# One written order for the first steps of a layer norm, Fourier mixing and MLP kernel; the copies of x moved behind the first transposes

## The chip, the cores and the metric

The kernel runs on one core of a Trainium2 chip. The metric is the device time of one execution in microseconds (us); before the change three runs gave a median of 1219.32 us. Five engines take part, each with its own queue that it works off in order: PE (TensorE, matmuls and the transposes made with matmuls), DVE (VectorE), ACT (ScalarE), POOL (GpSimd), and SP, which issues DMAs. POOL issues DMAs too.

## What is computed

```python
x = A_x                                   # 2048 x 576, f32
xn = _layernorm(x, axis=-1)
a, b = xn @ dft_hid_re.T, xn @ dft_hid_im.T
y = dft_seq_re @ a - dft_seq_im @ b       # 2048 x 2048 matrices
h = relu(xn @ w1)                         # w1: 576 x 4608
out = x + y + h @ w2                      # w2: 4608 x 576
```

Every f32 operand is carried as two f16 numbers, a high part and a low part (the value less its high part), and a product is three f16 matmuls (high by high, high by low, low by high). The products of the second layer and of the Fourier part are made in 2 x 2 blocks with seven multiplications instead of eight, which is why there are sums and differences of blocks as well.

## The kernel before

The 2048 rows of x are 16 tiles of 128 rows, tile 0 to 15, in four groups of four. The 4608 columns of the hidden layer are nine blocks of 512, taken as two pairs of 256. The main loop runs over steps `n` = (block `b`, group `g`), 36 of them: in step n the first layer of (b, g) and the second layer of the step before it stand interleaved. This change concerns what comes before step n = 3, that is block 0 with groups 0, 1 and 2.

A tile of x goes through this path. Its mean and variance (`stats`: two `bn_stats`, one `bn_aggr`, a square root on ACT, four short DVE operations). The normalized f32 value (`normalize`, L302 on DVE or L300 on ACT) and its f16 high part (L303 on ACT). The low part (`remainder`, L309 and L312, 64 and 512 columns, on POOL or DVE). Then ten 128 x 128 transposes: tiles 0 to 3 with matmuls (`transposes`, L332 and L336) and two copies out of PSUM on ACT (`copies`, L343 and L346); tiles 4 to 15 with one transposing DMA each from SP (`transposes_dma`, L326), for which 128 columns are copied once more first (L324 on POOL or L322 on ACT). Normalized tiles share four buffers in turn (tile t takes buffer t modulo 4).

The weights: `max_w1` and `power_w1` find a power-of-two scale of a block of w1, `split_w1` (L230 high, ACT; L231 low, DVE) makes the two f16 parts; `sum_w2`, `power_w2`, `split_w2`, `sums_w2` do it for w2. A scale needs a maximum over the 128 partitions. In block 0 that goes over PE (`power_pe`). In every later block it is POOL's `partition_all_reduce` (L168), after which DVE makes the scale (L171, L172, L176) and ACT and DVE the parts. In the middle of the first steps stands one more such reduction, of a constant into a tile that nobody reads (L1003, tile `none`).

The first layer of group 0 and half of group 1 is made tile by tile (`tile_by`, 14 matmuls of 128 columns), the rest with 512 columns (`mlp1`, L388). `mlp1_out` and `pair_out` make the f16 parts of the relu values and of their sums (L441 to L464); their last operation, on DVE, is the low part of four sums (L464). `mlp2` makes seven products a group (L699, 12 matmuls each, two PSUM banks in turn), ACT or DVE takes them out (L714, L718), and POOL adds four finished quarters to DRAM tiles `spill` with an accumulating DMA (L721). Those tiles start as copies of x (`copy_x`, L909).

What sets the order. Before step 3, each engine's queue is arranged by a scheduler from the order in which the code stands and from extra constraints (`behind(key)`: not before a named instruction). From step 3 on nearly everything goes through `pinned`, which lets an instruction follow the one that was issued before it on PE, ACT and DVE. `fill(n)` puts matmuls on PE whose result is not used. `work()` takes the next piece of the preparation of block 1 from a list (`prepare_block(1)`).

Of the kernel before, what the change touches and what calls it, by code (L numbers as in the profile page):

```python
# [18 lines left out]
P = 128  # L19
S = 2048  # L20
D = 576
# [34 lines left out]
def kernel(  # L56
# [142 lines left out]
    def power_pe(s, p, m):  # L199

        n = m.shape[-1]
        ps = ps2.tile([P, 2, 512], F32, tag="ps2", name="pm")

        for c in range(n):
            nc.tensor.matmul(
                ps[:1, 0, c * P : (c + 1) * P], m[:, c : c + 1], ident.bitcast(BF16),
                start=True, stop=True,
            )
        top = small.tile([1, n], BF16, tag=f"top{n}", name="top")
        order["top"] = nc.vector.tensor_reduce(  # L210
            top, ps[:1, 0, : n * P].rearrange("p (n f) -> p n f", f=P), AX.X, ALU.max
        ).ins
        order["pm"] = nc.tensor.matmul(ps[:, 1, :n], ones, top, start=True, stop=True).ins
        half = small.tile([P, n], F32, tag=f"half{n}", name="half")
        nc.vector.tensor_scalar(half, ps[:, 1, :n], 2.0**-107, 2.0**6, ALU.max, ALU.mult)
        nc.vector.tensor_scalar(
            s.bitcast(I32), half.bitcast(I32), EXPONENT, EXPONENT,
            ALU.bitwise_and, ALU.bitwise_xor,
        )
        nc.vector.tensor_scalar(  # L220
            p.bitcast(I32), half.bitcast(I32), EXPONENT, None, ALU.bitwise_and
        )
# [4 lines left out]
    def split(hi, lo, src, s):  # L227

        return (
            nc.scalar.activation(hi, src, AF.Copy, scale=s).ins,  # L230
            nc.vector.scalar_tensor_tensor(lo, src, s, hi, ALU.mult, ALU.subtract).ins,  # L231
        )
# [15 lines left out]
    def stats(ts, after=None, late=None):  # L248

        n = len(ts)  # L250
        mv = small.tile([P, n, 2], F32, tag=f"mv{n}", name=f"mv{ts[0]}")
        sts = [small.tile([P, 2, 6], F32, tag="st", name=f"st{t}", bufs=4) for t in ts]
        for t, st in zip(ts, sts):
            for j in range(2):
                with behind(after):
                    nc.vector.bn_stats(st[:, j, :], acc[t][:, j * EH : (j + 1) * EH])  # L256
                yield
        for i, st in enumerate(sts):
            order["stats"] = nc.vector.bn_aggr(mv[:, i], st.rearrange("p a b -> p (a b)")).ins
            yield  # L260
        r0, u, r, sh = (
            small.tile([P, n], F32, tag=f"{a}{n}", name=f"{a}_{ts[0]}") for a in ("r0", "u", "r", "sh")
        )
        m, v = mv[:, :, 0], mv[:, :, 1]
        stt = nc.vector.scalar_tensor_tensor
        order["root", ts[0]] = nc.scalar.activation(u, v, AF.Sqrt, bias=eps, scale=HALF**2).ins
        with behind(late):
            nc.vector.reciprocal(r0, u)
            stt(r0, v, EPS, r0, ALU.add, ALU.mult)
        yield  # L270
        with behind(late):
            stt(r0, r0, HALF**2, u, ALU.mult, ALU.add)
        yield
        with behind(late):
            nc.vector.reciprocal(r, r0)
        yield
        with behind(late):
            order["sh", ts[0]] = stt(sh, m, -1.0, r, ALU.mult, ALU.mult).ins
        for i, t in enumerate(ts):
            means[t], factors[t], shifts[t] = mv[:, i, 0:1], r[:, i : i + 1], sh[:, i : i + 1]  # L280

    def weave(steps, *others):

        others = list(others)
        for _ in steps:
            if others:
                others.pop(0)()
        for f in others:
            f()
# [3 lines left out]
    def normalize(t, eng=nc.vector, after=None):  # L293
        stage = dbufs[t % 4]
        xn = xns[t] = stage[:, :D]

        xs = xss[t] = stage[:, D : 2 * D + P // 2].bitcast(F16)
        with behind(after):
            if eng is nc.scalar:
                nc.scalar.activation(xn, acc[t], AF.Identity, bias=shifts[t], scale=factors[t])  # L300
            else:
                eng.tensor_scalar(xn, acc[t], means[t], factors[t], ALU.subtract, ALU.mult)  # L302
            order["N", t] = nc.scalar.activation(  # L303
                xs[:, :D], acc[t], AF.Identity, bias=shifts[t], scale=factors[t]
            ).ins

    def remainder(t, eng):
# [4 lines left out]
        order["E", t] = eng.tensor_tensor(  # L312
            xs[:, D + REM : 2 * D], xn[:, : KM * P], xs[:, : KM * P], ALU.subtract
        ).ins

    def transposes_dma(t, eng):

        xs = xss[t]
        g, c = divmod(t, TG)
        again = xs[:, 2 * D :], xs[:, D - P : D]  # L320
        if eng is nc.scalar:
            eng.activation(*again, AF.Copy)  # L322
        else:
            order["again"] = eng.tensor_copy(*again).ins  # L324
        with behind("td"):
            order["td"] = nc.sync.dma_start_transpose(xT[g][:, :, c * P : (c + 1) * P], xs).ins  # L326

    def transposes(t):
        xs = xss[t]
        pt = ps2.tile([P, 2, 1024], F16, tag="ps2", name=f"pt{t}")  # L330
        for k in range(NKX):
            nc.tensor.transpose(  # L332
                pt[:, k // 8, (k % 8) * P : (k % 8 + 1) * P], xs[:, k * P : (k + 1) * P], ident
            )

        nc.tensor.transpose(pt[:, 1, P : 2 * P], xs[:, D - P : D], ident)  # L336
        return pt

    def copies(t, pt, after=None):
        g, c = divmod(t, TG)  # L340
        dst = xT[g][:, :, c * P : (c + 1) * P]
        with behind(after):
            nc.scalar.activation(  # L343
                dst[:, :8, :], pt[:, 0, :].rearrange("p (k t) -> p k t", t=P), AF.Copy
            )
            nc.scalar.activation(  # L346
                dst[:, 8:, :], pt[:, 1, : 2 * P].rearrange("p (k t) -> p k t", t=P), AF.Copy
            )

# [70 lines left out]

    def mlp1_out(b, g, i, pa, pb, after=None, last=None, late=False):  # L430

        h, st = new_h(b, g, i), stages[i].rearrange("p (k t) -> p k t", t=GH)
        stt = nc.vector.scalar_tensor_tensor
        a11, a21, a12, a22 = pa[:, :GH], pa[:, GH:], pb[:, :GH], pb[:, GH:]
        r21, s1, s2, s3, s4 = (st[:, n] for n in range(5))
        with behind(after):  # L440
            nc.scalar.activation(r21, a21, AF.Relu)  # L441
        both = pb.rearrange("p (a t) -> p a t", t=GH)
        for q, src in ((A11, a11), (slice(A12, A22 + 1), both)):
            hi, lo = (h[:, n, q] for n in range(2))
            with behind(after):
                order["hi"] = nc.scalar.activation(hi, src, AF.Relu).ins
                order["hl"] = stt(lo, src, 0.0, hi, ALU.max, ALU.subtract).ins  # L447

        def values():
            with behind(last or after):  # L450
                stt(s3, a11, 0.0, r21, ALU.max, ALU.subtract)
                stt(s1, a22, 0.0, r21, ALU.max, ALU.add)
                stt(s2, a22, 0.0, s3, ALU.max, ALU.subtract)
                stt(s4, a12, 0.0, s2, ALU.max, ALU.subtract)

        hi, lo = (h[:, n, S1 : S4 + 1] for n in range(2))

        def high():
            with behind("free" if late else None):
                order["s"] = nc.scalar.activation(hi, st[:, 1:], AF.Copy).ins  # L460

        def low(key="vfree"):
            with behind(key if late else last):
                order["lo"] = nc.vector.tensor_tensor(lo, st[:, 1:], hi, ALU.subtract).ins  # L464

        if last:
            return lambda: (values(), high(), low())
        values()
        if late:
            return high, low  # L470
        high()
        low()

# [248 lines left out]
    def max_w1(b, f):  # L725
# [6 lines left out]
        with behind("vfree" if b else ("sh", 1) if f > 1 else None):  # L732
# [13 lines left out]
    def power_w1(b, i):  # L746
# [4 lines left out]
        else:  # L751
            power_pe(s, p, mx["b", i])

    def split_w1(b, f):
# [6 lines left out]
        split(w[:, 0, k], w[:, 1, k], raws["w1", b, i][:, k], sc["w1", b][:, i : i + 1])  # L761
# [22 lines left out]
    def sum_w2(b, i, after=("root", 4)):  # L784
# [5 lines left out]
        with behind("free" if b >= BB else None if b else after):  # L790
# [4 lines left out]
    def power_w2(b):  # L795
# [3 lines left out]
        else:  # L799
            m = small.tile([P, NQ], BF16, tag="mb2", name=f"mb2_{b}")  # L800
            with behind("stats"):
                order["cast"] = nc.vector.tensor_copy(m, mx["w2", b]).ins
            power_pe(sc["w2", b], pw["w2", b], m)
        p1 = pw["w1", b]
        pp = cell("pp")
        nc.vector.tensor_tensor(pp, p1, pw["w2", b], ALU.mult)
        m = cell("mp", 1)
        nc.vector.tensor_reduce(m, pp, AX.X, ALU.max)
        inv = cell("inv", 1)
        nc.vector.tensor_scalar(  # L810
            inv.bitcast(I32), m.bitcast(I32), EXPONENT, None, ALU.bitwise_xor
        )
        sc["w2", b] = cell("sw2")
        nc.vector.tensor_scalar(sc["w2", b], p1, inv, None, ALU.mult)  # L814
        us[b] = cell("ub", 1)
# [918 lines left out]
```

## Time and profile before

| | before |
|---|---|
| median of three runs | 1219.32 us (1219.3 to 1219.45) |
| the profiled execution | 1219.38 us, its span 1217.6 us |
| PE busy | 1207.3 us, 99% of the span |
| DVE, ACT, POOL busy | 1012.2, 718.1, 162.8 us |
| first matmul of the first layer | 12.25 us from the span's start |
| first layer of step 3 begins | 82.80 us |
| granted clock of PE | 1.0 throughout |

PE is the bound: after step 3 has begun it has no gaps in the windows shown below. So a change of the first steps moves the time by as much as it moves the moment at which PE goes on without gaps.

### The profile page before, as it was taken

How to read it: one execution, taken by the hardware profiler on the slowest of the kernel's cores; microseconds unless marked ns; L12 is line 12 of the kernel's file. 1: busy time of each engine (PE TensorE's matmuls, PEld its weight loads, DVE VectorE, ACT ScalarE, POOL GpSimd, SP SyncE). 2: the span in 40 equal slices, each digit the busy share in tenths (PEclk: the TensorE clock that was granted, in tenths of full speed). 3: DMA queues.
4: the chain of work that ended last, by engine and by line, in shares of the span. 5: the costliest groups of instructions: out<-in, count | busy, mean ns of one | idle time of the engine just before them, and what ended most of it. 6: DMA issues, size and time to landing. Idle time of an engine off the chain costs nothing.

```text
span 1217.6 us, 24548 instructions
## 1 busy us (share of the span) xinstructions
PE 1207.3 (99%) x10173; PEld 955.8 (78%) x10173; DVE 1012.2 (83%) x1647; ACT 718.1 (59%) x1073; POOL 162.8 (13%) x205
## 2 busy tenths in 40 slices
PE   8999999999999999999999999999999999999998
PEld 7666657888888888888888888877777777777776
DVE  8998999887787788788877877678898978787875
ACT  5756556876676766767666767555644433433332
POOL 2531211111121212111111211100000000000000
PEclk9999999999999999999999999999999999999999
DMA  8984545767666675666676666520165254534320
GB/s 318 212 153 106 93 89 121 155 138 161 157 143 158 141 176 124 146 152 149 137 164 157 126 161 161 92 31 1 66 208 174 80 178 140 175 109 149 99 89 20
DMA packets 84063, 164.64 MB, mean 135 GB/s; under 512 B 22640, under 2 KB 43632, under 8 KB 83952
## 3 DMA queue, kind: packets, MB, share of 16 engines
q1 hardware_dynamic: 61168, 120.61, 30.8%
q0 software_dynamic: 22784, 42.48, 24.0%
q8 instruction: 79, 1.29, 0.4%
q14 instruction: 32, 0.26, 0.1%
HBM read 110.76 MB, written 53.08 MB: 135 GB/s over the span
## 4 chain that ended last, share of the span: by engine, by line
PE 95%; DVE 3%; ACT 1%; DMA 0%; issue 0%; SPq 0%; ACTq 0%; DVEq 0%
PE p L699 30%; PE p L1634 27%; PE bank L604 23%; PE p L388 5%; PE U L1423 4%; PE W L1423 2%; PE bank L623 1%; PE V L1423 1%; DVE st L256 1%; DMA arena<-in_x_dram 0%; DVE arena L302 0%; DVE arena L231 0%; ACT arena L303 0%; DVE arena L464 0%; DVE arena L447 0%
## 5 line engine op out<-in xcount | busy, mean ns | idle before, releaser
L699 PE MATMUL p<-arena 128*128 128x288 f16 x3024 | 398.6, 286 | 0.9 <-DVE arena L718 0.9
L699 PEld LDWEIGHTS <-arena 128*128 128x128 f16 x3024 | 295.9, 98 | 76.5 <-issue 1.3
L1634 PE MATMUL p<-arena 128*128 128x288 f16 x2688 | 329.4, 286 | 0.0
L1634 PEld LDWEIGHTS <-arena 128*128 128x128 f16 x2688 | 263.0, 98 | 66.3
L604 PE MATMUL bank<-arena 128*128 128x256 f16 x2580 | 304.8, 273 | 0.0
L604 PEld LDWEIGHTS <-arena 128*128 128x128 f16 x2580 | 250.2, 98 | 37.5 <-issue 5.9
L230 ACT ACTIVATE arena<-arena,sc_c 128x1024 f16<-128x1024 f32 x112 | 128.5, 1148 | 189.9 <-PE p L1634 137.8
L721 POOL DMA_DIRECT2D spill<-arena x144 | 128.4, 897 | 553.6 <-DVE arena L718 480.6
L231 DVE SCALAR_TENSOR_TENSOR arena<-arena,sc_c 128x1024 f16<-128x1024 f32 x112 | 143.4, 1281 | 29.5 <-ACT arena L230 26.3
L714 ACT ACTIVATE arena<-p,c_ub 128x576 f32<-128x576 f32 x144 | 105.9, 736 | 43.0 <-PE p L699 38.8
L231 DVE SCALAR_TENSOR_TENSOR arena<-arena,c_sw 128x640 f16<-128x640 f32 (+2 forms) x118 | 96.3, 850 | 31.1 <-ACT arena L230 31.0
L718 DVE SCALAR_TENSOR_TENSOR arena<-p,c_ub,arena 128x576 f32<-128x576 f32 x108 | 87.9, 815 | 19.6 <-PE p L699 18.6
L632 DVE TENSOR_TENSOR arena<-bank,arena 128x512 f32<-128x512 f32 x84 | 57.9, 689 | 53.6 <-PE bank L604 52.5
L388 PE MATMUL p<-arena 128*128 128x128 f16 (+1 forms) x680 | 98.9, 300 | 1.6 <-ACT arena L343 0.7
L230 ACT ACTIVATE arena<-arena,c_sw 128x640 f16<-128x640 f32 (+2 forms) x118 | 88.9, 794 | 13.3 <-DVE c_sw L814 7.6
L629 ACT ACTIVATE arena<-bank 128x512 f32<-128x512 f32 x112 | 66.4, 593 | 51.3 <-PE bank L604 51.2
L1423 PEld LDWEIGHTS <-arena 128*128 128x128 f16 x738 | 71.6, 98 | 19.7 <-issue 1.9
L388 PEld LDWEIGHTS <-arena 128*128 128x128 f16 x680 | 52.3, 98 | 40.8 <-issue 3.6
L635 ACT ACTIVATE arena<-arena 128x512 f16<-128x512 f32 x84 | 52.9, 630 | 50.9 <-DVE arena L632 50.0
L1642 DVE SCALAR_TENSOR_TENSOR arena<-p,us_c,arena 128x288 f32<-128x288 f32 x112 | 57.5, 514 | 26.8 <-PE p L1634 26.4
L1219 ACT ACTIVATE arena<-arena 128x1024 f32<-128x1024 f32 x64 | 67.1, 1048 | 3.3 <-DMA arena<-in_cim_dram 2.4
L645 DVE TENSOR_TENSOR arena<-arena 128x1024 f16<-128x1024 f32 x56 | 68.2, 1218 | 0.3 <-ACT arena L641 0.3
(150 smaller groups left out, 1049.4 us busy)
## 6 DMA issues: line engine op xcount, KB each, us to landing
spill<-arena POOLq DMA_DIRECT2D x144, 288.0 KB, 5.0
arena<-in_cre_dram SPq DMA_DIRECT2D x64, 512.0 KB, 4.3
arena<-in_cim_dram SPq DMA_DIRECT2D x64, 512.0 KB, 4.8
arena<-in_w_dram SPq DMA_DIRECT2D x17, 640.0 KB, 5.9
arena<-in_w_dram SPq DMA_DIRECT2D x18, 576.0 KB, 3.7
arena<-spill SPq DMA_DIRECT2D x40, 144.0 KB, 2.2
arena<-in_x_dram SPq DMA_DIRECT2D x16, 288.0 KB, 7.4
spill<-in_x_dram SPq DMA_DIRECT2D x16, 288.0 KB, 5.6
```

What stands on the lines that cost most here:

```text
L230: nc.scalar.activation(hi, src, AF.Copy, scale=s).ins,
L231: nc.vector.scalar_tensor_tensor(lo, src, s, hi, ALU.mult, ALU.subtract).ins,
L388: order["m1"] = nc.tensor.matmul(ps[:, cols], w1s[b, i // 2][:, hl, i % 2 * KT + k], xT[g][:, kx, cols], start=(start and n == 0), stop=(s ...
L604: nc.tensor.matmul(ps[:, i], l, r, start=first and i == m == 0, stop=m == len(todo) - 1, skip_group_check=not first or i > 0,)
L645: order["lo"] = nc.vector.tensor_tensor(lo, stage[:, 1 + 2 * i :][:, :2], hi, ALU.subtract).ins
L699: order["pe"] = nc.tensor.matmul(ps[:, c], h[:, x, qa, c * P : (c + 1) * P], w[:, y, qb], start=first and i == 0 and j == 0, stop=i == NQ ...
L714: freed(nc.scalar.activation(o, ps, AF.Copy, scale=us[b]))
L718: add = nc.vector.scalar_tensor_tensor(o, ps, us[b], o, ALU.mult, ALU.add)
L721: nc.gpsimd.dma_start(spill[g, row, col], o, accum_op=ALU.add)
L1219: nc.scalar.activation(f, f, AF.Abs, scale=2.0**-10, accum_out=sums_c[:, n, q : q + 1])
L1423: nc.tensor.matmul(ps, l, r, start=first and m == 0, stop=m == len(todo) - 1, skip_group_check=not first,)
L1634: nc.tensor.matmul(ps, w[:, a, k], r[:, c, RQ[rq]], start=first and k == 0 and j == 0, stop=k == HK - 1 and j == 2, skip_group_check=not f ...
```

## The change

All that stands before step 3 is now one table of some 260 entries (a function and its arguments), worked off through `pinned`, and `pinned` holds POOL and SP to that order too while the table lasts. Operations that were one function are taken apart (`split_hi` and `split_lo`, `high_x`, `normal`, `low_x`, `again`, parts of `transposes` and `copies`), so that the table can place each on its own. The last step that had mixed code, n = 2, is in the table; the loop begins at 3.

```diff
+    tails, pinning = {}, [*ENGINES, mybir.EngineType.Pool, mybir.EngineType.SP]
...
+        for i in traced[n:]:
+            if i.engine in pinning:
+                tails[i.engine] = i
...
-    copy_x(0)
-    copy_x(1)
     warm = const.tile([P, 1], F32, name="warm")
...
-    fill(64)
...
-    fill(24)
-    T(0)
-    fill(10, xss[0])
...
-    with behind("again"):
-        nc.gpsimd.partition_all_reduce(const.tile([P, 1], F32, name="none"), eps, P, ReduceOp.max)
...
+    def low_x(t, eng):
         xn, xs = xns[t], xss[t]
         eng.tensor_tensor(
             xs[:, D : D + REM], xn[:, KM * P :], xs[:, KM * P : D], ALU.subtract
         )
...
+    for f, *a in (
...
+        (fill, 50),
...
+        (low_x, 15, GP),
...
+        pinned(f, *a)
...
-    for n in range(2, len(steps)):
+    for n in range(3, len(steps)):
...
-                normalize(t, after="free" if i == 3 else None)
-                remainder(t, nc.vector)
-                transposes_dma(t, nc.scalar)
```

Three moves besides the order itself. PE's unused matmuls go from 64 + 24 at the start and 32 wider ones between the first tiles to 50 + 4 at the start and 4 more. Of the normalized values, those of tiles 0, 1, 3, 7, 9, 13, 14 and 15 leave DVE for ACT, and the one of tile 10 comes back to DVE; of the low parts, tile 0 and tiles 13, 14 and 15 go from DVE to POOL. The copies of x for groups 0 and 1 stand on SP behind the transposing DMAs of tiles 4 to 11 (before: ahead of them), those of groups 2 and 3 behind those of tiles 12 to 15 (before: ahead).

The first place is POOL at the end of the first steps. `L168 ISA top` (and L1003's) is the reduction over partitions, a bare `ISA` is an instruction that changes the library that POOL runs, and `spill` DMAs are finished quarters of the second layer. Before:

```order
L324 COPY arena<-arena 128x128
L1003 ISA
L1003 ISA none<-eps 128x1
L721 DMA spill_00_70<-arena 256x1x288
...
L721 DMA spill_10_76<-arena 256x1x288
L168 ISA top<-c_mw_1314 128x1 x2
L721 DMA spill_00_78<-arena 256x1x288
```

And now, from the same kind of copy on (the pair of L320 and L323 stands there three times, for tiles 15, 13 and 14):

```order
L334 COPY arena<-arena 128x128
L168 ISA
L168 ISA top<-c_mw_1143 128x1
L668 DMA spill_00_74<-arena 256x1x288
L320 ISA
L320 TENSOR_TENSOR arena<-arena 128x64
L323 TENSOR_TENSOR arena<-arena 128x512
...
L668 DMA spill_11_77<-arena 256x1x288
L168 ISA
L168 ISA top<-c_mw_1143 128x1
```

There was one bare `ISA` behind POOL's last low part of x, ahead of the unread reduction; now there are three, as low parts stand between the two reductions of block 1's w1.

The second place is DVE at the end of the first steps: `half`, `c_sw` and `c_pw` are the scale of w1 that is made from the reduction's `top`; the TENSOR_TENSOR of 128x4x256 is the low part of four sums. Before:

```order
L718 SCALAR_TENSOR_TENSOR arena<-p_0_1_3_1256,c_ub,arena 128x2x288
L464 TENSOR_TENSOR arena<-arena 128x4x256
L162 TENSOR_REDUCE c_mf<-arena 128x1 x3
L739 TENSOR_REDUCE c_mw_1314<-c_mf 128x1
L162 TENSOR_REDUCE c_mf<-arena 128x1
L171 TENSOR_SCALAR half<-top 128x1
L739 TENSOR_REDUCE c_mw_1314<-c_mf 128x1
L172 TENSOR_SCALAR c_sw_1315<-half 128x1
L176 TENSOR_SCALAR c_pw_1316<-half 128x1
L171 TENSOR_SCALAR half<-top 128x1
```

And now, at the second of the two reductions:

```order
L665 SCALAR_TENSOR_TENSOR arena<-p_0_1_3_1190,c_ub,arena 128x2x288
L438 SCALAR_TENSOR_TENSOR arena<-p_0_2_3_1166,arena 128x2x256
L440 SCALAR_TENSOR_TENSOR arena<-p_0_2_3_1166,arena 128x256
L171 TENSOR_SCALAR half<-top 128x1
L172 TENSOR_SCALAR c_sw_1144<-half 128x1
L176 TENSOR_SCALAR c_pw_1145<-half 128x1
L444 TENSOR_TENSOR arena<-arena 128x4x256
L235 SCALAR_TENSOR_TENSOR arena<-arena,c_sw_1144 128x640 x2
L444 TENSOR_TENSOR arena<-arena 128x4x256
L665 SCALAR_TENSOR_TENSOR arena<-p_0_2_1_1301,c_ub,arena 128x2x288
```

Both low parts of the sums of group 2 (L444, tile names `p_0_2`) stand behind DVE's wait for the second reduction; before, they stood ahead of both.

The third place is ACT in the first twenty microseconds: `pt` is a tile of transposes in PSUM, L343 and L346 the copies out of it (now L353), L230 (now L232) a high part of w1, L303 (now L316) the high part and L310 the normalized value of a tile of x. Before:

```order
L303 ACTIVATE arena<-arena,sh_214,r_213 128x576
L266 ACTIVATE u_248<-mv_242,eps 128x1
L230 ACTIVATE arena<-arena,c_sw_219 128x640
L343 ACTIVATE arena<-pt_281 128x8x128
L346 ACTIVATE arena<-pt_281 128x2x128
L230 ACTIVATE arena<-arena,c_sw_219 128x640
L303 ACTIVATE arena<-arena,sh_250,r_249 128x576
```

And now:

```order
L316 ACTIVATE arena<-arena,sh_142,r_141 128x576
L310 ACTIVATE arena<-arena,sh_142,r_141 128x576
L288 ACTIVATE s_228<-mv_226,eps 128x1
L353 ACTIVATE arena<-pt_214 128x4x128
L232 ACTIVATE arena<-arena,c_sw_205 128x640
L353 ACTIVATE arena<-pt_214 128x6x128
L316 ACTIVATE arena<-arena,sh_231,r_230 128x576
L310 ACTIVATE arena<-arena,sh_231,r_230 128x576
```

The normalized values of tiles 0 and 1 have come to ACT, and the transposes of a tile are copied in two parts, high ones first.

More of the change, by code (lines that the diff above doesn't have):

```diff
@@ L246, in behind, with begin @@
         return tc.issue_after(order[key]) if key in order else nullcontext()
-    def stats(ts, after=None, late=None):
+    mvs, sts, chains = {}, {}, {}
+    def begin(ts):
         n = len(ts)
[L251 to L262, printed above, removed]
-        )
+        mv = small.tile([P, n, 2], F32, tag=f"mv{n}", name=f"mv{ts[0]}", bufs=3)
+        for i, t in enumerate(ts):
+            mvs[t] = mv[:, i]
+        chains[ts[0]] = chain(ts, mv)
```

829 lines of the change are left out of this document (516 added, 313 removed).

## Prediction

> **What bounds the kernel now.** I read the page first, its engine shares.
>
> ```profile
> PE 1207.3 (99%) x10173; PEld 955.8 (78%) x10173; DVE 1012.2 (83%) x1647; ACT 718.1 (59%) x1073; POOL 162.8 (13%) x205
> ```
>
> PE is busy for all but 10 us of the span, so the first steps count only through the time at which PE has them done. Then the windows of 10 us, for where it loses time:
>
> ```profile
> core 0: us, PE busy (x) PEld busy (x) DVE busy (x) ACT busy (x) POOL busy (x), PEclk, DMA share, GB/s
> 10.00:20.00 10.00, 8.20 (x100) 6.28 (x97) 9.40 (x35) 6.58 (x11) 1.61 (x2) 1.00 1.04 409
> 50.00:60.00 10.00, 9.45 (x65) 6.19 (x64) 10.00 (x21) 5.92 (x10) 3.47 (x2) 1.00 0.82 261
> 60.00:70.00 10.00, 9.67 (x68) 6.42 (x66) 10.00 (x30) 5.24 (x9) 3.28 (x3) 1.00 0.79 107
> 80.00:90.00 10.00, 10.00 (x63) 5.57 (x61) 9.61 (x21) 4.47 (x6) 3.67 (x5) 1.00 0.98 142
> ```
>
> From 80 us on PE is full. From 50 to 70 us DVE is full and PE has small gaps. The timeline of PE gives the marks that I compare with:
>
> ```profile
> 12.25 1.10 PE L388 MATMUL p<-arena 128*128 128x128 f16 x14
> 47.46 6.21 PE L388 MATMUL p<-arena 128*128 128x512 f16 x28
> 57.16 4.57 PE L699 MATMUL p<-arena 128*128 128x288 f16 x36 [0.55 <-DVE arena L718]
> 61.57 1.03 PE L388 MATMUL p<-arena 128*128 128x512 f16 x4
> 62.92 1.63 PE L699 MATMUL p<-arena 128*128 128x288 f16 x12 [0.33 <-DVE arena L718]
> 64.39 2.32 PE L388 MATMUL p<-arena 128*128 128x512 f16 x10
> 82.80 2.97 PE L388 MATMUL p<-arena 128*128 128x512 f16 x13
> 89.05 3.10 PE L699 MATMUL p<-arena 128*128 128x288 f16 x24
> ```
>
> The first layer begins at 12.25; that of group 2 at 47.46; group 0's last second-layer product ends at 64.4, where the next row begins; step 3's first layer begins at 82.80; group 2's third product at 89.05, with PE full on both sides of it. All sums are made against this execution, 1219.38 us, 1.8 more than its span and 0.06 above the median of 1219.32, inside the runs' spread.
>
> **Part 1: a gain at the front.** In the new order ACT paces the first 25 us. Its pieces and waits in before's timeline:
>
> ```profile
> 10.48 0.81 ACT L230 ACTIVATE arena<-arena,c_sw 128x640 f16<-128x640 f32 x1
> 11.19 1.00 ACT L343 ACTIVATE arena<-pt 128x1024 f16<-128x1024 f16 x1
> 12.10 0.37 ACT L346 ACTIVATE arena<-pt 128x256 f16<-128x256 f16 x1
> 12.36 0.82 ACT L230 ACTIVATE arena<-arena,c_sw 128x640 f16<-128x640 f32 x1
> 16.69 1.02 ACT L343 ACTIVATE arena<-pt 128x1024 f16<-128x1024 f16 x1 [2.75 <-PE pt L336]
> 20.98 1.63 ACT L303 ACTIVATE arena<-arena,sh,r 128x576 f16<-128x576 f32 x2 [1.37 <-DVE sh L278]
> 23.73 0.30 ACT L266 ACTIVATE u<-mv,eps 128x4 f32<-128x4 f32 x1 [1.12 <-DVE mv L259]
> 25.10 1.16 ACT L791 ACTIVATE arena<-arena 128x1152 f16<-128x1152 f32 x1
> 26.25 0.86 ACT L303 ACTIVATE arena<-arena,sh,r 128x576 f16<-128x576 f32 x1
> ```
>
> From start to start a split takes 0.71, the copies of a tile's ten transposes 1.17 (0.91 and 0.26), a normalization 0.8 (half of 1.63), a sum of w2 1.15. Between the first split and tile 4's high part the table has on ACT four splits (2.9), 3.6 tiles of copies (4.2), five normalizations (4.0), two square roots (0.3 each, 0.6 at most; I take 0.4) and one sum of w2 (1.15): 12.65. The scale that starts them comes about when it did: tile 0's statistics no longer wait behind w1's maximum, and w1's maximum now waits behind them. So tile 4's high part stands at 10.48 + 12.65 = 23.1 instead of 26.25, 3.1 earlier. From there the eight low parts of tiles 4 to 11 still go through POOL, and the transposing DMAs behind them, so group 2's first layer comes 3.1 earlier too.
>
> After it PE's two waits on DVE (0.55, 0.33) can go, as DVE has seven normalizations and four low parts less; and the four matmuls of row 61.57 (0.86) now stand behind group 0's last product. That product thus ends 3.1 + 0.88 + 0.86 = 4.8 earlier, at 59.6; 4.0 of it is a gain. Ends for that gain: 0, if DVE's written order holds what ACT has ready, and 6.1, if all of ACT's waits above (2.75, 1.37, 1.12) vanish and the 0.88 too. I take 4.0, as the sum of ACT's own rows gives it.
>
> The copies of x for groups 0 and 1 cost nothing behind the transposing DMAs as long as they land before POOL's first accumulating DMA, some 10 us later; if not, POOL waits for them, and that is inside part 2's chain. Those of groups 2 and 3 stand behind the last transposing DMA and are needed after step 3's start.
>
> PE also loses the unused matmuls between the tiles. What these rows show:
>
> ```profile
> 2.00:3.00 1.00, 1.00 (x13) 1.00 (x11) 1.00 0.88 289
> 5.00:6.00 1.00, 1.00 (x22) 1.00 (x20) 1.00 0.77 249
> ```
>
> In a microsecond PE did 13 of the unused matmuls at 2 us and 22 at 5 us, at the same recorded clock of 1.00: it starts slow and becomes fast. If it turns slow again in the new idle time, the some 140 small matmuls and transposes up to 25 us take 0.077 instead of 0.045 each, at most 4.5 more; most would lie beside ACT's 12.65, so I take 0. [...]
>
> **Part 2: a loss at the end of the first steps.** POOL now changes its library three times there. Before did it once, at L1003, where nobody waited:
>
> ```profile
> L1003 POOLq MODIFY_POOL_CONFIG  x2: 9/9/9, 43.3 to 43.3; - x2
> L1003 POOL PARTITION_ALL_REDUCE none<-eps x1: 2466/2466/2466, 49.6 to 49.6; - x1
> 49.61 2.47 POOL L1003 PARTITION_ALL_REDUCE none<-eps  x1 [6.54 <-issue]
> 82.89 0.35 POOL L168 PARTITION_ALL_REDUCE top<-c_mw  x1 [0.71 <-DVE c_mw L739]
> 35.58 0.31 POOL L309 TENSOR_TENSOR arena<-arena 128x64 f16<-128x64 f32 x1 [0.90 <-DVE arena L302]
> 36.95 0.29 POOL L324 COPY arena<-arena 128x128 f16<-128x128 f16 x1
> 78.31 1.08 POOL L721 DMA_DIRECT2D spill<-arena  x1 [4.01 <-DVE arena L718]
> arena<-arena SPq DMA_TRANSPOSE x12, 3.4
> 81.53 0.74 ACT L714 ACTIVATE arena<-p,c_ub 128x576 f32<-128x576 f32 x1 [0.73 <-PE p L699]
> 79.32 1.21 DVE L464 TENSOR_TENSOR arena<-arena 128x1024 f16<-128x1024 f32 x1
> 85.22 3.26 DVE L231 SCALAR_TENSOR_TENSOR arena<-arena,c_sw 128x640 f16<-128x640 f32 x4
> ```
>
> The change of library is at 43.3, the reduction starts at 49.61, and POOL waits for nothing that the profile shows: 6.3. That first reduction takes 2.47, the next one 0.35. A low part takes 1.37 (35.58 to 36.95), an accumulating DMA 1.1. The change back to the tensor operations' library isn't timed in before; its price lies between 0 and 6.3, and I take 6.3, the row of the same instruction.
>
> From the end of group 0's last product at 59.6, in POOL's written order: ACT takes it out behind activations that stand queued (0.74 and about 1.0) 61.3; its DMA and a copy (1.1, 0.3) 62.7; library 69.0; first reduction (2.47) 71.5; DMA 72.6; library 78.9; three low parts 83.0; DMA 84.1; library 90.4; second reduction 92.9. Behind that reduction DVE stands: the scale (about 0.3), the low part of the sums (1.2), two low splits of w1 (half of 3.26, 1.6), the second low part of the sums (1.2), that is 97.2. Group 2's third product multiplies these sums, so it begins at 97.2 instead of 89.05: 8.1 late. Queued behind the same wait on DVE are the evictions of step 3; ACT stands too, at the high splits. Meanwhile step 3's first layer waits for tiles 13 to 15, whose DMAs follow the low parts (83.0) one by one and take 3.4 each to land, some 88 for the last; the first layer's two pieces ahead of the third product take 6.2 (82.80 to 89.05) and still fit ahead of 97.2. PE never catches up, as it is full after it. Sum: 1219.38 + 8.1 = 1227.5.
>
> [...]
>
> **The rivals.**
>
> Changes of library after the first cost nothing that counts, so the gain stays: faster. For it: the 6.3 could be one loading of code that then stays; against it: the instruction stands there three times, and at 43.3 nothing but it can explain the 6.3. Without any such cost POOL's chain from 59.6 is 97.2 less 18.9 less two first-call surcharges of 2.1, 74.1; it hides under 89.05 - 4.0. It decides where three loads together come under 85.0 - 74.1 = 10.9, some 3.6 each. Time: 1219.4 - 4.0 = 1215.4. If only the first load costs, the chain ends at 97.2 - 12.6 - 2.1 = 82.5, but the low parts of tiles 13 to 15 end at 76.7 then and their DMAs land near 81.5, where PE would be ready at 82.8 - 4.0 = 78.8: 2.7 of the 4.0 are lost, 1218.1.
>
> Only the change back is free: the chain is 6.3 shorter, 90.9, 1.9 late: 1221.3.
>
> PE turns slow and DVE's order holds up the front, so there is no gain, and POOL's chain starts 4.0 later: 1231.5. For it: the unused matmuls were there between the tiles; against it: ACT, not PE, paces that stage.
>
> **How the numbers follow.** The forecast, three paid changes, has 0.60, the last rival on top of it 0.08 more. The change back free has 0.10, only the first load paid 0.09, none paid 0.13. About 0.2% (2.4 us) is what a measurement of this kernel can tell from no change, so the same is 1216.9 to 1221.8. Slower by more: the 0.68 and a fourth of the change back being free, 0.70. The same: the rest of that and most of the one load, 0.15. Faster: no cost, and a piece of the one load, 0.15. The range reaches from 1217.5, which takes in the case of one load, to 1231.5; left out are the case without cost and little above.
>
> **What would show it.** In the changed profile: the first layer of group 2 at about 44.4; group 0's last product ending near 59.6; on POOL three gaps of 6.3 put down to issue, ahead of L168, L320 and L168 again; DVE's L171 idle for several us behind the second L168; PE idle ahead of step 3's first layer and ahead of group 2's third product at about 97. I am wrong if POOL's gaps behind the first are short, or if group 0's last product is not earlier than 64.4.

## The result and the profile after

| | before | after |
|---|---|---|
| median, us | 1219.31 (1219.21 to 1219.45, 4 runs) | 1232.99 (1231.88 to 1233.66, 4 runs) |
| profiled execution, us | 1219.38 | 1231.88 |
| its span, us | 1217.6 | 1230.1 |

The changed kernel takes 1.0111 times as long, with a 95% interval of 1.0094 to 1.0129. The forecast was 1227.5, its range ended at 1231.5: the sign was right, the size too small by 5.5 us. The profiled execution after is the fastest of its four, 1.1 us below their median. The two profiled executions differ by 12.5 us, and all of it is there at one place: group 2's third product begins at 101.53 instead of 89.05.

PE in the changed kernel's timeline (start, duration, line, operand shapes, number of matmuls, and in brackets the idle time ahead with what ended it):

```profile
47.05 6.30 PE L383 MATMUL p<-arena 128*128 128x512 f16 x28 [0.49 <-DMA arena<-arena]
62.02 3.19 PE L383 MATMUL p<-arena 128*128 128x512 f16 x14
76.20 6.24 PE L646 MATMUL p<-arena 128*128 128x288 f16 x36 [2.10 <-ACT arena L661]
83.27 3.10 PE L646 MATMUL p<-arena 128*128 128x288 f16 x24 [0.83 <-ACT arena L661]
93.89 4.36 PE L383 MATMUL p<-arena 128*128 128x512 f16 x13 [7.52 <-issue]
101.53 3.10 PE L646 MATMUL p<-arena 128*128 128x288 f16 x24
```

Group 2's first layer stands at 47.05 (47.46 before), group 0's last product ends at 62.02 (64.39 before). Up to there the new order leads. Then PE stands still three times (2.10, 0.83, 7.52 us), and step 3's first layer, at 93.89, is 11.1 us behind the 82.80 of before; its thirteen matmuls take 4.36 us instead of 2.97.

POOL in the same timeline, with rows from the views of lines L339 (the transposing DMAs; the second is from its list of who waited for them, in us), L168 and L320 (SPq and POOLq are the sequencers of SP and POOL: shortest, median and longest duration in ns, then first and last start):

```profile
64.65 1.73 POOL L334 COPY arena<-arena 128x128 f16<-128x128 f16 x1
72.91 0.38 POOL L168 PARTITION_ALL_REDUCE top<-c_mw  x1 [6.53 <-issue]
73.17 1.28 POOL L668 DMA_DIRECT2D spill<-arena  x1
82.48 0.30 POOL L320 TENSOR_TENSOR arena<-arena 128x64 f16<-128x64 f32 x1 [8.03 <-issue]
86.60 1.23 POOL L668 DMA_DIRECT2D spill<-arena  x1
94.67 0.38 POOL L168 PARTITION_ALL_REDUCE top<-c_mw  x1 [6.84 <-DMA spill<-in_x_dram]
L339 SPq DMA_TRANSPOSE arena<-arena x4: 1357/1866/2664, 65.2 to 88.3; - x4
PE p L383: 7.5, 1
L168 POOLq MODIFY_POOL_CONFIG  x4: 475/971/1467, 65.1 to 87.7; - x4
L320 POOLq MODIFY_POOL_CONFIG  x4: 11/269/528, 0.8 to 74.1; - x4
```

Three gaps, 6.53, 8.03 and 6.84 us, each behind a change of library (65.1, 74.1, 87.7). The last is put down to a DMA, but the change stands at 87.7 and the reduction follows 7.0 later, much as in the first case (7.8, with a copy still running at its start). The low parts of tiles 13 to 15 stand between the second and the third gap (82.48 to 86.6), their transposing DMAs behind them (the last starts at 88.3), and step 3's first layer behind those: the view of L339 names it as what waited, with the 7.5 us that PE's row leaves to "issue".

What waits for the two reductions, on DVE and ACT:

```profile
73.32 0.16 DVE L171 TENSOR_SCALAR half<-top 128x1 f32<-128x1 f32 x1 [4.24 <-POOL top L168]
73.70 0.83 ACT L232 ACTIVATE arena<-arena,c_sw 128x640 f16<-128x640 f32 x1 [5.57 <-DVE c_sw L172]
95.08 0.15 DVE L171 TENSOR_SCALAR half<-top 128x1 f32<-128x1 f32 x1 [11.71 <-POOL top L168]
98.13 1.22 DVE L444 TENSOR_TENSOR arena<-arena 128x1024 f16<-128x1024 f32 x1
```

Behind the first reduction DVE stands still for 4.24 us and ACT for 5.57; the eviction for which PE waits 2.10 at 76.20 stands on ACT behind that. Behind the second, DVE stands still for 11.71 us and has the sums' low parts done at 99.35. PE takes them at 101.53, so DVE isn't the last wait any more; step 3's first layer is. The windows by stage (busy time of PE, PEld, DVE, ACT, POOL, then the granted clock of PE, DMA share and GB/s):

```profile
10.00:20.00 10.00, 7.54 (x62) 5.97 (x63) 9.90 (x32) 8.43 (x13) 4.73 (x7) 0.50 1.04 410
70.00:80.00 10.00, 7.91 (x43) 4.65 (x41) 5.14 (x11) 4.78 (x8) 1.54 (x2) 0.83 0.30 44
90.00:100.00 10.00, 6.11 (x23) 2.25 (x24) 4.88 (x9) 2.17 (x3) 2.68 (x3) 0.66 1.08 270
```

PE's clock, 1.00 in each of these stretches before, is 0.50 at the front, where fewer unused matmuls stand between PE's waits, 0.83 from 70 to 80 us, and 0.66 around the long wait. DVE is busy 9.90 of 10 us at the front, more than ACT. Three rows of ACT and one of DVE show what the front waits for:

```profile
15.99 0.87 ACT L316 ACTIVATE arena<-arena,sh,r 128x576 f16<-128x576 f32 x1 [1.09 <-DVE sh L298]
21.29 1.24 ACT L353 ACTIVATE arena<-pt 128x1280 f16<-128x1280 f16 x1 [0.79 <-PE pt L348]
25.05 2.37 ACT L316 ACTIVATE arena<-arena,sh,r 128x576 f16<-128x576 f32 x3
14.24 1.12 DVE L292 SCALAR_TENSOR_TENSOR q<-mv,q 128x2 f32<-128x2 f32 x1
```

Tile 4's high part, the first of the three at 25.05, is 1.2 earlier than before's 26.25; 23.1 was predicted.

### The profile page after: what moved, and what is told of

Same layout as the page of the kernel before. It is cut to its first block, busy times and chain, and to the rows that moved or that the text cites. A ratio compares the mean times of both kernels' runs of the same rounds, so it can differ in the third digit from the quotient of the medians.

```text
span 1230.1 us, 24431 instructions
## 1 busy us (share of the span) xinstructions
PE 1209.7 (98%) x10117; PEld 956.0 (78%) x10117; DVE 1008.5 (82%) x1632; ACT 723.9 (59%) x1078; POOL 168.5 (14%) x212
## 4 chain that ended last, share of the span: by engine, by line
PE 93%; issue 3%; POOL 2%; DVE 1%; DMA 1%; SPq 0%; POOLq 0%; ACT 0%
PE p L646 28%; PE p L1811 27%; PE bank L551 23%; PE p L383 6%; PE U L1600 4%; PE W L1600 2%; PE bank L570 1%; PE V L1600 1%; POOL arena L323 1%; DMA arena<-arena 0%; POOL spill L668 0%; POOL arena L334 0%; DVE st L270 0%; DMA spill<-in_x_dram 0%; DVE c_mf L162 0%
## 5 line engine op out<-in xcount | busy, mean ns | idle before, releaser
L232 ACT ACTIVATE arena<-arena,sc_c 128x1024 f16<-128x1024 f32 x112 | 128.5, 1148 | 189.8 <-PE p L1811 137.5
L383 PE MATMUL p<-arena 128*128 128x128 f16 (+1 forms) x680 | 102.6, 309 | 9.2 <-issue 7.5
L232 ACT ACTIVATE arena<-arena,c_sw 128x640 f16<-128x640 f32 (+2 forms) x118 | 89.2, 793 | 22.1 <-DVE c_pw L176 11.0
```

The costliest lines, as they stand in the source:

```text
L383: order["m1"] = nc.tensor.matmul(ps[:, cols], w1s[b, i // 2][:, hl, i % 2 * KT + k], xT[g][:, kx, cols], start=(start and n == 0), stop=(s ...
```

## Experiments

Medians are of the runs of each kernel; ratios are to the kernel before, run on the same chip. Where a time is set against that of another experiment or of after, the two medians may come from different chips.

### Where the loss comes from

**e1: the three low parts back on DVE.**

```diff
-        (low_x, 15, GP),   # and 13, 14
+        (low_x, 15, V),    # and 13, 14
```

> The changed kernel, with one thing put back: the low parts of tiles 13, 14 and 15 are made on DVE and not on POOL. POOL then changes its library once at the end of the first steps (ahead of the first reduction) instead of three times. Theory 'library' (each change costs POOL 6.5 to 8.4 us in the open): two of the three go, step 3's first layer and group 2's third product no longer wait; 10 to 13 us less than the changed kernel's 1233, so 1219 to 1222, with DVE still idle some 4 us ahead of its first scale of block 1. Rival 'front' (the new order of the first tiles with its slow PE makes the loss): at least 1228.

1223.12 us, ratio 1.0031 (1.0021 to 1.004): 9.9 us of the loss are gone with three low parts on another engine. It is 1.1 above the range expected, since one change of library stays, and PE waits for what stands behind it:

```profile
73.99 0.38 POOL L168 PARTITION_ALL_REDUCE top<-c_mw  x1 [6.99 <-issue]
77.27 3.10 PE L646 MATMUL p<-arena 128*128 128x288 f16 x24 [2.55 <-ACT arena L661]
```

**e2: that one hidden as well.** An unread reduction behind tile 11's low part, as before had one, and POOL's last two copies on ACT so that the library stays.

```diff
+        (preload,),         # behind (low_x, 11, GP)
-        (again, 13, GP),    # and 14
+        (again, 13, A),     # and 14
```

> As the kernel with the low parts of 13, 14, 15 on DVE, and besides the unread reduction is put behind tile 11's low part on POOL again, and the extra column copies of tiles 13 and 14 go from POOL to ACT, so that the one change of library lies where POOL is idle. Theory 'library': nothing of the loss is left and the front's gain of about 1.5 us (group 0's last product) shows: 1217 to 1219. Rival 'front': at least 1225.

1218.96 us, ratio 1.0000 (0.999 to 1.0009). The load is there, at a place where nobody waits:

```profile
50.23 0.38 POOL L945 PARTITION_ALL_REDUCE none<-eps  x1 [6.49 <-issue]
62.25 3.19 PE L383 MATMUL p<-arena 128*128 128x512 f16 x14
79.30 3.10 PE L646 MATMUL p<-arena 128*128 128x288 f16 x24 [0.55 <-DVE arena L665]
82.23 2.97 PE L383 MATMUL p<-arena 128*128 128x512 f16 x13
88.49 3.10 PE L646 MATMUL p<-arena 128*128 128x288 f16 x24
```

So the whole loss comes from the changes of library and what follows from them. e2 also shows what the new order is worth without them: group 0's last product ends 2.14 earlier than before, less the 0.86 of the four matmuls put behind it 1.3; a new wait for DVE (0.55) takes part of that, and the third product is 0.56 earlier than before.

**e3: the loss alone.** The kernel before with only its low parts 13 to 15 on POOL.

```diff
-                remainder(t, nc.vector)
+                remainder(t, GP if t > 12 else nc.vector)
```

> The kernel before, with one thing of the change alone: the low parts of tiles 13, 14 and 15 are made on POOL and not on DVE (DVE has 3 us less to do, POOL changes library two more times). Theory 'library': step 3's first layer comes about 5 us late and the scales of block 1 some 8 us: 1224 to 1228. Rival 'front': no loss, 1218.5 to 1219.5.

1229.55 us, ratio 1.008 (1.0065 to 1.0095), 1.5 above the range expected. The change back and the second change to the reduction's library stand in POOL's timeline (the first of the rows names DVE, whose operation had ended just before, so not all of its 9.02 need be the change). PE's layer comes 7.7 late and takes 5.70 us instead of 2.97, with a granted clock of 0.68 from 90 to 100 us:

```profile
75.48 0.30 POOL L309 TENSOR_TENSOR arena<-arena 128x64 f16<-128x64 f32 x1 [9.02 <-DVE arena L454]
91.85 0.72 POOL L168 PARTITION_ALL_REDUCE top<-c_mw  x2 [7.63 <-issue]
90.48 5.70 PE L388 MATMUL p<-arena 128*128 128x512 f16 x13 [7.75 <-issue]
```

**e8: only the first load hidden.** The changed kernel with e2's unread reduction and copies; the low parts 13 to 15 stay on POOL.

> The kernel after (1232.99 us) with an unread reduction on POOL behind tile 11's low part, and the copies 13 and 14 on ACT instead of POOL so that the reduction's code stays; the low parts 13 to 15 stay on POOL, so POOL changes its code twice more, behind the first reduction and ahead of the second. Theory each load has its price: the first reduction is 4 to 5 us earlier (68.4 instead of 72.9), low parts, their transposing DMAs and step 3's first layer follow by as much: 1228 to 1229.5 us. Theory the pair of loads alone binds: the 12.5 us hang on the loads that the three low parts cause and the first one was hidden by other waits: within 1 of 1233. Theory the loads overlap: all of the loss goes, 1219 to 1221.

1229.23 us, ratio 1.0081 (1.0068 to 1.0095): 3.8 less than after, within what the first theory gave, and out of the reach of the others. With the 9.9 of e1 that is 13.7; taking both away gave 14.0 (e2). Set against the kernel before on the same chip, the kernel after is 13.7 slower, the first change alone (e1) costs 3.9, the other two (e8) cost 10.0. So the prices add up. The rows of the two that remain in e8:

```profile
79.17 0.29 POOL L320 TENSOR_TENSOR arena<-arena 128x64 f16<-128x64 f32 x1 [8.13 <-issue]
91.59 0.38 POOL L168 PARTITION_ALL_REDUCE top<-c_mw  x1 [7.07 <-DMA spill<-in_x_dram]
```

**e9 and e11: PE's clock behind the long wait.** The changed kernel with unused 128x128 matmuls ahead of step 3's first layer, 66 in e9 and 122 in e11.

```diff
             ps.append(new_ps1(b, g, 0))
+            if (b, g) == (0, TG - 1):
+                for _ in range(66):     # e11: 122
+                    nc.tensor.matmul(ps[0][:, :P], idle, idle, start=True, stop=True)
```

> The kernel after (1232.99 us) with 66 unused 128x128 matmuls on PE ahead of step 3's first layer, in the 7.5 us in which PE stands still there; everything else as it is. Theory clock: the layer then takes 2.97 us instead of 4.36, step 3's third product begins 1.4 us earlier (DVE is ready for it at 99.35, 2.2 us ahead): 1231.3 to 1232.0 us. Rival: the slow stretch costs nothing because the third product waits for DVE, or the unused matmuls delay the layer: 1232.7 to 1234.

e9: 1232.53 us (1231.86 to 1234.56), ratio 1.0109 (1.0093 to 1.0124). It missed its aim: 66 matmuls last 3.85 us, 4.58 us of idle time stay, and the layer is slow again (5.71, with a granted clock of 0.71 from 90 to 100 us).

```profile
86.64 3.85 PE L416 MATMUL p<-idle 128*128 128x128 f16 x66
95.07 5.71 PE L383 MATMUL p<-arena 128*128 128x512 f16 x13 [4.58 <-issue]
```

> The kernel after (1232.99 us) with 122 unused 128x128 matmuls on PE ahead of step 3's first layer; at the 0.058 us that each of 66 took there (3.85 us), they last 7.1 us and fill the 7.5 us in which PE stands still. Theory clock: the layer takes 2.97 us instead of 4.36, and step 3's third product begins 1.4 us earlier: 1231.3 to 1232.0 us. Rival: nothing is gained, since DVE or a transfer ends as late: 1232.5 to 1233.5; or the matmuls run past the arrival of tiles 13 to 15 and delay the layer, up to 1234.

e11: 1230.93 us (1230.47 to 1231.95), ratio 1.0099 (1.0085 to 1.0113), 2.1 less than after; 1.0 to 1.7 were expected. Each set against the kernel before on its own chip, the difference is 1.8.

```profile
85.36 6.97 PE L416 MATMUL p<-idle 128*128 128x128 f16 x122
94.22 2.97 PE L383 MATMUL p<-arena 128*128 128x512 f16 x13 [1.88 <-issue]
100.47 3.10 PE L649 MATMUL p<-arena 128*128 128x288 f16 x24
```

The layer begins 0.3 later than in after, takes 2.97 again at a granted clock of 1.00, and the third product is 1.06 earlier. So the slow clock is a cost of its own, on top of the wait ahead of it: 1.4 in after's profiled run, 2.7 in e9's and e3's. The trace shows this; the times show it less well, since the runs of e11 and after come from different chips, their ranges (up to 1231.95 and from 1231.88) touch, and the intervals of their ratios overlap. The length of a wait alone doesn't decide over the clock: behind the 2.10 us at 76.20 in after, 36 matmuls of the second layer took 6.24 instead of the 4.57 of 65.04 (granted clock 0.56 from 76 to 78 us), while behind 2.55 in e1 and 3.08 in e11 the clock stayed 1.00, and 24 matmuls took 3.10 as elsewhere.

### Where the gain at the front went

**e4: the copies of x alone.** The kernel before with the copies for groups 0 and 1 behind the transposing DMAs.

```diff
-    copy_x(0)
-    copy_x(1)
 ...
+    copy_x(0)      # behind tile 11's transposing DMA
+    copy_x(1)
```

> The kernel before, with another thing of the change alone: the copies of x of groups 0 and 1 stand on SP behind the transposing DMAs of tiles 4 to 11. My costing at nothing: 1219.3 within 0.5. Rival (the copies' traffic delays the transposing DMAs, or they come too late for POOL's first accumulating DMA): 1 us or more to either side.

1220.51 us, ratio 1.0012 (1.0003 to 1.0022): about 1.2 slower. But the edit changed more than the copies. Before step 3 a scheduler arranges each engine's queue from the order in which the code stands, and here it gave ACT and DVE another order. ACT's two activations of L446 stand at 32.05 in before (first row) and behind three others at 36.41 in e4 (second row), while step 3's first layer is at 83.67 instead of 82.80:

```profile
32.05 0.87 ACT L446 ACTIVATE arena<-p 128x256 f16<-128x256 f32 x2
36.41 0.84 ACT L446 ACTIVATE arena<-p 128x256 f16<-128x256 f32 x2
83.67 2.97 PE L388 MATMUL p<-arena 128*128 128x512 f16 x13
```

In e4 DVE's operation behind those activations starts at 36.81; the scale ahead of it (L814) took 1.19 us beside a low part on POOL, 0.44 in before, where it began 0.41 ahead of such a low part's end. Up to 35 us e4 is 0.5 ahead of before, at 42.35 DVE is 0.88 late, and the first moved copy is issued only at 43.99. From there the lag doesn't grow: PE is 0.87 late at 83.67. So the loss in this trace comes from the other order on ACT and DVE, not from the copies' transfers.

**e6: the copies put back ahead, in the new order.** e2 with `copy_x(0)` and `copy_x(1)` behind the loads again.

> The kernel with the preloaded reduction, the copies 13 and 14 on ACT and the low parts 13 to 15 on DVE (1218.96 us), with the copies of x for groups 0 and 1 back in the place before: ahead of the transposing DMAs, right behind the loads. Theory copies: as in the kernel before with the copies moved alone (plus 1.2 us), their bytes behind the transposes lengthen the DMAs of 50 to 80 us that something waits for, so this kernel is 0.8 to 1.6 us faster: 1217.4 to 1218.2 us. Rival: in the new order nothing waits for those DMAs (the first steps have slack behind group 1), or the copies delay tiles 4 to 7 instead: within 0.5 of 1219.0, or slower by up to 1.

1219.25 us, ratio 1.0000 (0.9991 to 1.0009), against e2's 1218.96. The rival holds: in the new order the copies' place makes no difference that can be measured. Here the written order holds, so this edit moves the copies alone, as e4's did not.

**e7: tile 0's low part on DVE**, as before, on top of e2.

```diff
-        (low_x, 0, GP),
+        (low_x, 0, V),
```

> The kernel with the preloaded reduction, the copies 13 and 14 on ACT and the low parts 13 to 15 on DVE (1218.96 us), with tile 0's low part on DVE, as before the change, instead of POOL. Theory: tile 0's low part waits on POOL for code (it begins at 8.95 us though its normal value is there at 7.68) and stretches a DVE operation from 0.16 to 0.9 us, so on DVE the first layer begins about 1 us earlier and the whole front with it: 1217.9 to 1218.5 us, tile 4's high part 0.5 to 1 earlier. Rival: DVE is busy over 9 of 10 us there and 1.4 us more of work on it pushes its chain: 1219.0 to 1220.4 us, tile 4's high part 0.3 to 1.4 later.

1218.66 us, ratio 0.9995 (0.9986 to 1.0003): 0.3 less than e2, below what the rival gave and 0.2 above the theory's range. Tile 4's high part is at 24.73 (25.24 in e2). POOL's first change of library, at 0.8 us, isn't in the way any more, and the same small DVE operation that took 0.91 in after takes 0.14:

```profile
10.27 0.14 DVE L292 SCALAR_TENSOR_TENSOR q<-mv,q 128x1 f32<-128x1 f32 x1
```

**e5: unused matmuls back in PE's gaps**, on e2.

```diff
-        (fill, 50),
+        (fill, 64),
 ...
-        (fill, 4),
+        (fill, 16),
 ...         # and 8, 3, 6, 10, 5 more between the transposes and products of tiles 0 and 1
```

> The kernel with the preloaded reduction, the copies 13 and 14 on ACT and the low parts 13 to 15 on DVE (1218.96 us), with unused matmuls put back into PE's gaps of the first 20 us (50 to 64, 4 to 16, and 32 more in four places). Theory clock: the new order's front gains only about 2 us on PE because PE's clock is 0.50 from 10 to 20 us; with the clock kept up, the first layer's pieces between 12 and 22 us take about 1.8 us less, and group 0's last product ends at 60 to 61 instead of 62.25: 1217.0 to 1218.2 us. Rival cover: PE waits in those 10 us for ACT, DVE and POOL, so a faster PE only waits longer: group 0's last product stays within 0.3 of 62.25 and the time within 0.5 of 1219.0. Rival in the way: the unused matmuls stand in front of work that is ready, 0.3 to 1 us slower.

1219.23 us, ratio 1.0000 (0.9991 to 1.0008). PE's clock came up to 0.83 from 10 to 20 us, and tile 4's high part didn't come earlier (25.36). Inconclusive: in the profiled run POOL began tile 0's low part only at 10.95, and ACT waited for the transposes behind it, which hides whatever the clock gave:

```profile
12.91 0.81 ACT L353 ACTIVATE arena<-pt 128x768 f16<-128x768 f16 x1 [2.40 <-PE pt L348]
```

**e10: e7 and e6 together.**

> The kernel with the preloaded reduction, the copies 13 and 14 on ACT and the low parts 13 to 15 on DVE, with tile 0's low part on DVE and the copies of x for groups 0 and 1 back ahead of the transposing DMAs, both. Alone the first gave 1218.66 us (ratio 0.9995) and the second 1219.25. Theory the gains of both places remain: 1218.0 to 1218.7 us, a little faster than the kernel before (1219.23). Rival: the front's lead of about half a microsecond is lost in the wait for DVE ahead of group 0's second product: 1218.9 to 1219.5.

1218.44 us, ratio 0.9995 (0.9987 to 1.0004): inside the range of the first theory, with an interval that still holds 1.

**e12: tile 1's low part on DVE too**, on e10.

```diff
-        (low_x, 1, GP),
+        (low_x, 1, V),
```

> The kernel with the preloaded reduction, the low parts 13 to 15 and tile 0's on DVE and the copies of x ahead (1218.44 us), with tile 1's low part on DVE too. Theory stretch: DVE's operation at 14 us takes 1.12 instead of 0.16 because POOL's 128x512 subtraction runs beside it, and ACT waits 1.09 for the shift behind it; without that low part on POOL the wait is 0.1 to 0.3, and tile 4's high part is 0.5 to 0.9 earlier (24.62 now): 1217.6 to 1218.2 us. Rival: the low part's 0.87 us on DVE, which is busy 9.9 of 10 us there, or PE at half clock, takes it back: tile 4's high part within 0.3, the time within 0.4 of 1218.44.

1218.67 us, ratio 0.9999 (0.999 to 1.0008). The operation does shrink, and ACT's wait for the shift is gone. But PE, at clock 0.50 from 10 to 20 us, now makes ACT wait 1.44 for transposes (0.79 in e10), a wait of 0.47 for DVE is new, and tile 4's high part is at 25.10, 0.5 later than in e10. The time is within the rival's range: those two waits take back what the first one gave.

```profile
14.18 0.14 DVE L292 SCALAR_TENSOR_TENSOR q<-mv,q 128x2 f32<-128x2 f32 x1
21.52 1.24 ACT L353 ACTIVATE arena<-pt 128x1280 f16<-128x1280 f16 x1 [1.44 <-PE pt L348]
```

**e13: e12 with unused matmuls in PE's gaps**, 50 more up to 17 us, now that no low part of these tiles is on POOL.

> The kernel e12 with 50 more unused matmuls in PE's gaps of the first 17 us, so that its clock stays up (0.5 from 10 to 20 us without). Theory clock: ACT's wait of 0.79 for PE's transposes goes as well, tile 4's high part is 0.3 to 0.8 earlier than in e12: 0.3 to 0.8 us faster than e12, and with e12's theory 1217.0 to 1217.8 us, 0.1 to 0.2% under the kernel before. Rival: DVE paces these steps whatever PE's clock: within 0.3 of e12. Rival in the way: the unused matmuls delay ready work: 0.3 to 1 us slower than e12.

1218.31 us, ratio 0.9995 (0.9987 to 1.0004): 0.4 less than e12, barely past the rival's 0.3, with ranges of the runs that overlap, so the times don't decide. The trace does for the front: the clock is 1.00 from 10 to 20 us, ACT's wait for the transposes is gone, and tile 4's high part is at 23.72, 1.4 earlier than in e12 and near the 23.1 of the prediction. Yet group 2's first layer is at 46.78, only 0.7 earlier than before. ACT, POOL, PE and two windows of e13:

```profile
23.72 2.37 ACT L316 ACTIVATE arena<-arena,sh,r 128x576 f16<-128x576 f32 x3
37.29 1.92 ACT L232 ACTIVATE arena<-arena,c_sw 128x864 f16<-128x864 f32 x2 [1.36 <-DVE c_sw L773]
40.79 0.84 POOL L334 COPY arena<-arena 128x128 f16<-128x128 f16 x1 [2.21 <-ACT arena L316]
46.78 6.33 PE L383 MATMUL p<-arena 128*128 128x512 f16 x28 [0.44 <-DMA arena<-arena]
20.00:30.00 10.00, 8.94 (x154) 8.37 (x150) 9.85 (x33) 8.93 (x16) 4.45 (x8) 1.00 1.07 294
30.00:40.00 10.00, 9.36 (x148) 8.51 (x149) 9.96 (x31) 7.76 (x13) 6.92 (x13) 1.00 1.09 172
```

A lead of 2.5 us at tile 4 shrinks to 0.7 within 23 us, in which DVE (third pair of numbers) is busy 9.85 and 9.96 of 10 us (9.50 and 8.40 before). The rows show one chain that eats the lead. ACT has the split of w2 (L232) ahead of tile 11's normalization and high part, and waits 1.36 us for the scale that DVE makes for it. POOL waits 2.21 us for that high part and ends tile 11's low part at 43.27; before, where ACT made its last high part of these tiles ahead of the split of w2, POOL's last low part ended at 42.83. PE then waits for the transposing DMA. e7, e10 and e13 have the lowest medians, each 0.6 to 0.7 under that of the kernel before on their chip; no interval leaves out 1, so no gain is shown.

## Why the prediction was right in its sign and too small

**The changes of library: right.** All three are paid, and with what follows from them they are the whole loss (e2). The rivals in which only some cost are out: e8 took away the first and gained 3.8, e1 the other two and gained 9.9. The forecast's 6.3 came from one row of before (L1003); that a second change, and the change back, would cost as much was the author's estimate, which no run had shown. In its place the runs showed, for every change at the end of the first steps, gaps of 6.5 to 7.6 ahead of the reduction (6.53 in after, 7.63 in e3) and 8.0 to 8.5 on the way back (8.03 in after, 8.52 in e9; 9.02 in e3, where the row names DVE). Ahead of the unread reduction the gaps are 5.8 to 6.5 (5.83 in e8, 6.49 in e2).

**The length of POOL's chain: right as a sum, by errors that cancel.** From the end of group 0's last product to the end of DVE's work 37.6 us were predicted, 37.3 measured (62.02 to 99.35). The change back took 8.4 (74.1 to 82.48) instead of 6.3, the upper bound that the prediction gave it; the first reduction behind a load took 0.38, so the surcharge of 2.1 from before's row isn't a property of the load. The copies and eviction ahead of the first load took 4.4 instead of 3.1. That the sum came out is luck.

**"Group 0's last product ends 59.6": mis-sized.** It ended at 62.02, so the gain was 1.5 and not 4.0, and POOL's chain began 2.4 later. The step that failed is "ACT paces the first 25 us": other engines made ACT wait. ACT's own work was right: 14.57 us lie between its first split and tile 4's high part, 12.65 were summed, and its two waits (1.09 for DVE, 0.79 for PE) are the difference. The first comes from a DVE operation that POOL's low part holds up (gone in e12), the second from PE's clock of 0.50 (gone in e13). So "slow PE: I take 0" failed too; a part of the last rival, slow PE and DVE's order at the front, was true. The next step, "group 2's first layer comes 3.1 earlier too", failed as well: it came 0.4 earlier, with tile 4 1.2 earlier, and in e13 0.7 with tile 4 2.5 earlier. In e13 the written order on ACT, behind a scale from DVE, holds tile 11; DVE is full from 20 to 40 us and a likely bound there, but no run took work off it or changed that order, so this part stays open. What was to come behind it did: the two waits on DVE are gone, and from group 2's first layer to group 0's last product it takes 14.97 us instead of 16.93, 1.96 less, where 1.74 were predicted.

**"Still fit ahead of 97.2": wrong.** The third product waited for step 3's first layer, not for DVE (99.35). The low parts ended at 86.65 instead of 83.0, mostly by the late start of the chain. From there to the layer's start went 7.2 us, where 5.0 were taken, from a landing time of 3.4, the median over all twelve transposing DMAs of before. The four of this stretch take longer, a median of 4.7 in before's view of DMAs from 60 to 97 us, and 5.8 in after's:

```profile
arena<-arena SPq DMA_TRANSPOSE x4, 5.8
```

And the layer ran at a lowered clock: 4.36 instead of 2.97 (e11). Together the product is at 101.53, 4.3 later than predicted: 2.15 by DVE's end (99.35 for 97.2), 2.18 by the layer behind it. The remaining 1.1 of the 5.5 is the distance from the profiled execution to the median. The same layer took 5.70 in e3 and e8 and 5.71 in e9, 1.3 more than in after's trace; that this is the 1.1 isn't shown.

**The copies of x cost nothing: holds** in the new order (e6). In the old order e4 lost 1.2, but it changed the order on ACT and DVE too, and its trace puts the loss there.

## What to carry to other kernels

On POOL, count changes of kind, not instructions: three low parts put between two reductions cost two changes of library and some 10 us (9.9 by e1, 10.0 by e8), where DVE does one in 0.8 (64.02 to 64.83 in e8). Here a change cost nothing only where POOL was idle anyway, which an unread reduction at an idle place arranged (its gap: 6.49 in e2, 5.83 in e8). When summing a new order by one engine's work, look up which other engines are full in the windows, and follow the last tile's chain, not only the first one's: a lead of 2.5 us at tile 4 was gone at tile 11. A wait in front of PE can have a second price, a lowered clock behind it: 1.4 to 2.7 us for one layer here. When moving one piece of code in a kernel whose queues a scheduler arranges, compare the order on every engine before laying the difference to the piece (e4).

## What was not expected of the hardware

A small DVE operation that began while POOL's 128x512 subtraction ran was in several rows held until that ended: 1.12 us for a 128x2 operation with two tensor inputs at 14.24, beside POOL's 1.17 from 14.19 (after; both end at 15.36), 0.14 with that subtraction on DVE (e12). One with a single input was held too: L751's cast of 128x2 took 0.90 at 28.60 in after, beside POOL's 1.16 from 28.31; the same cast took 0.25 at 30.79 in before (L802 there), with no such subtraction beside it. Others were not held: L442, which reads PSUM, took its 0.41 at 36.07 in after, inside POOL's 1.16 from 35.31, and L290, which doesn't, 0.15 at 30.35, inside POOL's 1.16 from 29.69. What decides which of them is held isn't shown. With operations of 0.14 us the price lies in what waits behind: in after ACT waited 1.09 for the shift behind the one at 14.24.

POOL's very first change of library is at 0.8 us, and tile 0's low part behind it began late and not always alike: at 8.95 in after, where the row puts the wait to issue, and at 10.31 in e2 and 10.95 in e5, where it names ACT. What sets that isn't shown.
